# Attention and two feed-forward blocks on one core: when the first block's W34 parts are made, in which order its second products are queued, and where the x splits stand

## The chip, the cores and the metric

The kernel runs on one NeuronCore of one Trainium2 chip, as one program. The metric is the device time in microseconds. The kernel before took 2330.16 us, the median of 3 runs (2330.05 to 2332.1).

TensorE (PE in the profile) multiplies; VectorE (DVE), ScalarE (ACT) and GpSimd (POOL) split, add and evacuate; the sync engine (SP) issues the DMAs.

## The reference

```python
x = attention(q, k, v, tau)             # 4 x 8 heads, 576 tokens, 64 wide -> 2304 tokens x 512
x = ((x @ w1) * (x @ w2)) @ w3 @ w_out  # first block, weights in float64
P = sinkhorn(exp(x @ w_gate))           # 8 rounds, 2304 x 8
out = sum over e of P[:, e] * (relu(x @ e1[e]) @ e2[e])   # 8 experts, 512 -> 1024 -> 512
```

The kernel multiplies `w3 @ w_out` once beforehand and calls the result W34. The first block is then `((x @ w1) * (x @ w2)) @ W34`.

## The kernel before, in words

**Split numbers.** Each fp32 operand of a product is split into two fp32r parts, high and low (`xh`/`xl`, `w1h`/`w1l`, `w2h`/`w2l`, `hh`/`hl`). A product of two split operands is three matmuls: high by high, high by low, low by high. The high part is a copy on ACT, the low part a subtraction on DVE or POOL.

**Units.** The tokens are three superblocks of 768. The first block (24 units) goes superblock by superblock, eight units each: a, b, a, b, ... An a-unit is a quarter of `x @ w1`, the b-unit behind it the same quarter of `x @ w2`. Units are numbered from 0, so even ones are a and odd ones b; units 8, 16 and 24 open a superblock, and what happens around them is called a turn here. From unit 24 on there are 96 expert units of the same build.

**Slots.** A unit has seven slots (Strassen-Winograd). In each, `mm1` issues six matmuls of 384 columns into one of two PSUM banks (`px` for slots 0, 2, 4, `py` for 1, 3, 5, 6), then `pop` issues some second products, then `evac`/`combine` reads the bank: p, u, v and three or four results. In an a-unit the results stay in `ca`. In a b-unit each result c is multiplied by `ca` (the "product c", L652), ACT copies its high part `hh` and DVE makes its low part `hl` (L654). These steps wait in `self.later` and are issued one and two slots after, the last three behind slot 6.

**Second products.** At the end of a b-unit `queue_b` queues its 48 matmuls with W34: 24 of 256 columns into two `ye` banks, then 24 of 512 columns into four others. `pop` spreads them over the 16 shares of the next a- and b-unit (slot 5 has two shares). PE executes all of this in the order of issue.

**W34's parts.** `prep2` makes `w2h` on ACT at slot 3 and `w2l` on DVE (L566) at slot 5, and then issues the load of the next raw piece but one. In the first block it is called in the b-unit, for that unit's own quarter.

**x splits.** At a turn the seven `xh`/`xl` pairs of the next superblock are made by `xsplit` (L585 on ACT, L586 on DVE). `SPLITS_AT` says behind which slot: positions 0 to 6 are the slots of the last unit, 7 to 13 those of the first unit of the next superblock. Split number k is used first by slot k of that unit, at position 7 + k.

**POOL** makes the next unit's `w1` parts in each unit: L531, L534, L537, L538, L541 and, longest, L543.

Of the kernel before, what the change touches and what calls it, by code (L numbers as in the profile page):

```python
# [24 lines left out]
SB = 768  # L25
# [2 lines left out]
QW = 2 * S + 128  # L28

SPLITS_AT = ((0, 0), (1, 1), (2, 2), (3, 3), (8, 4), (9, 5), (10, 6))  # L30

CONVERT = (1, 1, 1, 1, 1, 1, 1, 1, 0, 1, 1, 2, 2, 1, 1, 2, 1, 1)
PRODUCTS = (0, 1, 0, 1, 4, 0, 4, 2, 1, 1, 3, 1, 0, 3, 0, 3, 3, 3)
# [8 lines left out]
def f32(ap):  # L42
    return ap.bitcast(F32)
# [422 lines left out]
class Moe:  # L466
# [87 lines left out]
        self.raw2[u] = raw  # L554

    def prep2(self, u, part):
        if u not in self.raw2:
            return
        if part == 0:
            wh = self.pool2.tile([128, 2, DM], F32R, tag="w2h", name=f"w2h{u}", bufs=2)  # L560
            self.nc.scalar.activation(wh, self.raw2[u], AF.Copy)
            self.w2[u] = [wh]
        else:
            raw = self.raw2.pop(u)
            wl = self.pool2.tile([128, 2, DM], F32R, tag="w2l", name=f"w2l{u}", bufs=2)
            self.nc.vector.tensor_tensor(out=wl, in0=raw, in1=f32(self.w2[u][0]), op=ALU.subtract)  # L566
            self.w2[u].append(wl)
            self.load2()
# [101 lines left out]
    def queue_b(self, u):  # L670
        kind, s, j = self.units[u]
        hh, hl = self.hs.pop(u)
        wh, wl = self.w2.pop(u)
        prods = ((wh, hh), (wh, hl), (wl, hh))
        for m in range(2):
            for n in (2 * m, 2 * m + 1):
                out = self.yb[4 + m][:, 256 * (n % 2):256 * (n % 2) + 256]
                for f in range(2):
                    for i, (w, h) in enumerate(prods):
                        self.mm2(out, w[:, f, 128 * n:128 * n + 128], h[:, f, 0:256],  # L680
                                 j == 0 and n % 2 == 0 and f == 0 and i == 0, j == 3 and n % 2 == 1 and f == 1 and i == 2)
            if j == 3:
                self.queue.append((0, lambda m=m: self.nc.vector.tensor_copy(
                    self.x[:, 2 * m:2 * m + 2, SB * s:SB * s + 256],
                    self.yb[4 + m].rearrange("p (a b) -> p a b", a=2))))
        for n in range(4):
            for f in (1, 0):
                for i, (w, h) in enumerate(prods):
                    self.mm2(self.yb[n], w[:, f, 128 * n:128 * n + 128], h[:, f, 256:SB],
                             j == 0 and f == 1 and i == 0, j == 3 and f == 0 and i == 2)  # L690
            if j == 3:
                self.queue.append((0, lambda n=n: self.nc.scalar.activation(
                    self.x[:, n, SB * s + 256:SB * s + SB], self.yb[n], AF.Copy)))
# [44 lines left out]
    def gate(self, s, slot):  # L738

        ps = self.xy[0 if slot == 6 else 1]  # L740
        t0 = slot - 2
        for tc in (t0, t0 + 1):
            t = SB * s + 128 * tc
            for d in range(4):
                self.nc.tensor.matmul(ps[:, E * tc:E * tc + E], lhsT=self.x[:, d, t:t + 128], rhs=self.wg[:, d],
                                      start=d == 0, stop=d == 3, skip_group_check=True)

        def out():
            self.nc.scalar.activation(self.p[:, 6 * s + t0:6 * s + t0 + 2],
                                      ps[:, E * t0:E * t0 + 2 * E].rearrange("p (a b) -> p a b", a=2), AF.Copy)  # L750
        return out
# [34 lines left out]
    def run(self):  # L786
        units = self.units
        self.load1(0)
        self.load1(1)
        prep = self.prep1(0)  # L790
        for slot in range(7):
            if slot < 4:
                self.xsum(0, slot, self.nc.vector)
            self.xsplit(0, slot)
            if slot >= PD:
                next(prep, None)
            yield
        for _ in prep:
            pass
        sink = None  # L800
        gates = {8 * s + (12 if s + 1 < NSB else 9): s for s in range(NSB)}
        for u, (kind, s, j) in enumerate(units):
            nxt = units[u + 1] if u + 1 < len(units) else None
            while u == 1 and self.pool2 is None:
                yield
            if kind != "a":
                self.hs[u] = tuple(self.pool2.tile([128, 2, SB], F32R, tag=t, name=f"{t}{u}", bufs=2)
                                   for t in ("hh", "hl"))
            ahead = [units[min(u + i, len(units) - 1)][1] for i in range(5)]
            splits = dict(SPLITS_AT) if ahead[1] != s else {}  # L810
            if u and units[u - 1][1] != s:
                splits = {at - 7: slot for at, slot in SPLITS_AT}
            prep = self.prep1(u + 1)
            self.load1(u + 2)
            for slot in range(7):
                yield
                late, self.late = self.late[:2], self.late[2:]
                self.mm1(u, slot)
                gate = self.gate(gates[u], slot) if u in gates and slot in (2, 4, 6) else None
                self.pop(slot)  # L820
                if sink:
                    try:
                        sink.send(self.xy[1 if slot < 4 else 0])
                    except StopIteration:
                        sink = None
                self.evac(u, slot)
                if gate:
                    gate()
                    if u == 8 * NSB + 1 and slot == 6:
                        sink = self.sinkhorn()  # L830
                        next(sink)
                for f in late:
                    f()
                if slot in splits:
                    self.xsplit(ahead[1], splits[slot])
                next(prep, None)
                if slot == 5 and ahead[4] != s:
                    self.xsum(ahead[4], next(i for i in range(4) if ahead[3 - i] == s), self.nc.gpsimd)
                if slot in (3, 5):
                    self.prep2(u, (slot - 3) // 2)  # L840
            while self.later:
                self.later.pop(0)()
            if kind == "b":
                self.queue_b(u)
                self.left = (2 if nxt[0] == "a" else 1) * (6 + SHARE)
            elif kind != "a":
                self.queue_d(u)
                self.left = 6 + SHARE
        self.left = 0
        self.pop(6)  # L850
        for f in self.late:
            f()
# [61 lines left out]
```

## Time and profile before

| | us |
|---|---|
| span of the profiled execution | 2331.0 |
| its time | 2332.75 |
| median of the runs | 2330.16 |
| PE busy | 2247.0 (96%) |
| DVE busy | 1283.8 (55%) |
| ACT busy | 999.3 (43%) |
| POOL busy | 1179.2 (51%) |

The profiled execution is itself a run of the kernel, 2.59 us above the median of the others. A busy PE is an upper bound, since matmuls are pipelined and their ends are modelled: where rows follow each other, the distance of their starts is the pace. In the trace a wait stands in brackets behind the instruction that waited, with what ended it. The first block runs from about 474 to 805 us; the last second products of it end in the unit that starts at 804.72 us.

### The profile page before, as it was taken

The numbers are of one execution on the slowest core, as the hardware profiler recorded it, in microseconds if no ns is written. First come the engines' busy times: TensorE is split into PE (matmuls) and PEld (weight loads), VectorE is DVE, ScalarE is ACT, GpSimd is POOL, SyncE is SP. The second block draws the span as 40 slices with busy tenths as digits, with TensorE's granted clock in tenths as the row PEclk, the third lists the DMA queues.
The fourth block names the chain that finished last, engine by engine and source line by source line (L and its number), as shares of the span: only waits on it lengthen the run. The fifth ranks groups of instructions, "written<-read, shape, count | busy, mean of one in ns | idle before, by whom it ended". The sixth has DMA issues, their size and how long they took to land.

```text
span 2331.0 us, 32170 instructions
## 1 busy us (share of the span) xinstructions
PE 2247.0 (96%) x12544; PEld 2053.2 (88%) x12544; DVE 1283.8 (55%) x2207; ACT 999.3 (43%) x1853; POOL 1179.2 (51%) x1093
## 2 busy tenths in 40 slices
PE   6999999988989899999999999999999999999999
PEld 6899999878888888999999999999999899999998
DVE  6888888665555655544444644444444634444444
ACT  5877877633333333333333433333333443333332
POOL 3655555376666644444445644444446544444441
PEclk8999999989999999999999999999999999999999
DMA  5334443111111111221111121211221222112211
GB/s 141 101 117 122 122 125 116 62 69 70 64 51 59 46 55 55 73 73 66 61 73 73 69 86 73 73 65 63 73 73 59 95 73 73 64 64 73 73 61 48
DMA packets 52824, 177.73 MB, mean 76 GB/s; under 512 B 6592, under 2 KB 6592, under 8 KB 52672
## 3 DMA queue, kind: packets, MB, share of 16 engines
q1 hardware_dynamic: 52672, 175.68, 22.5%
q8 instruction: 98, 1.61, 0.3%
q14 instruction: 54, 0.44, 0.1%
HBM read 164.64 MB, written 11.01 MB: 75 GB/s over the span
## 4 chain that ended last, share of the span: by engine, by line
PE 87%; DVE 8%; issue 2%; ACT 2%; DMA 0%; SPq 0%; DVEq 0%; ACTq 0%
PE ye L667 37%; PE py L597 20%; PE px L597 15%; PE pv L225 4%; PE s L138 4%; PE t L183 2%; PE w L424 2%; DVE xl L586 1%; DVE nmx L143 1%; DVE c L652 1%; DVE p L158 1%; PE vs L207 1%; PE xt L239 1%; PE tt L194 0%; DVE c L641 0%
## 5 line engine op out<-in xcount | busy, mean ns | idle before, releaser
L543 POOL TENSOR_TENSOR w1l<-wt,w1h 128x1024 fp32r<-128x1024 f32 x120 | 290.8, 2423 | 326.3 <-ACT w1h L540 326.3
L667 PE MATMUL ye<-w2h,hl 128*128 128x512 f32 x1152 | 452.4, 393 | 0.0
L667 PE MATMUL ye<-w2h,hh 128*128 128x512 f32 x1152 | 451.5, 392 | 0.0
L667 PE MATMUL ye<-w2l,hh 128*128 128x512 f32 x1152 | 450.8, 391 | 0.0
L662 ACT ACTIVATE hh<-c 128x384 fp32r<-128x384 f32 x288 | 151.4, 526 | 615.0 <-DVE c L641 614.9
L538 POOL TENSOR_TENSOR w1l<-raw,w1h 128x256 fp32r<-128x256 f32 x120 | 92.0, 766 | 515.1 <-ACT w1h L532 515.1
L597 PE MATMUL py<-xh,w1h 128*128 128x384 f32 x960 | 325.3, 339 | 17.8 <-DVE c L641 12.2
L597 PE MATMUL py<-xh,w1l 128*128 128x384 f32 x960 | 324.1, 338 | 0.4 <-POOL w1l L543 0.4
L597 PE MATMUL py<-xl,w1h 128*128 128x384 f32 x960 | 324.3, 338 | 0.0
L597 PE MATMUL px<-xh,w1h 128*128 128x384 f32 x720 | 243.8, 339 | 3.7 <-DVE hl L663 3.4
L667 PEld LDWEIGHTS ye<-w2h,hl 128*128 128x128 f32 x1152 | 216.5, 188 | 32.5
L667 PEld LDWEIGHTS ye<-w2l,hh 128*128 128x128 f32 x1152 | 216.4, 188 | 32.5
L597 PE MATMUL px<-xh,w1l 128*128 128x384 f32 x720 | 243.1, 338 | 0.0
L597 PE MATMUL px<-xl,w1h 128*128 128x384 f32 x720 | 243.1, 338 | 0.0
L667 PEld LDWEIGHTS ye<-w2h,hh 128*128 128x128 f32 x1152 | 216.5, 188 | 24.0
L597 PEld LDWEIGHTS py<-xh,w1h 128*128 128x128 f32 x960 | 181.1, 189 | 43.1 <-DVE c L641 15.6
L597 PEld LDWEIGHTS py<-xl,w1h 128*128 128x128 f32 x960 | 181.5, 189 | 17.9
L624 DVE TENSOR_TENSOR u<-py,p 128x384 f32<-128x384 f32 x120 | 66.8, 556 | 215.9 <-PE py L597 215.0
L597 PEld LDWEIGHTS py<-xh,w1l 128*128 128x128 f32 x960 | 181.7, 189 | 0.9 <-POOL w1l L543 0.9
L531 POOL TENSOR_TENSOR wt<-raw 128x512 f32<-128x512 f32 x120 | 162.9, 1358 | 27.3 <-DMA raw<-w_a 12.3
L663 DVE SCALAR_TENSOR_TENSOR hl<-c,hh 128x384 fp32r<-128x384 f32 x288 | 164.6, 572 | 9.5
L662 ACT ACTIVATE hh<-px 128x384 fp32r<-128x384 f32 x96 | 47.4, 494 | 274.7 <-PE px L597 274.7
(138 smaller groups left out, 4584.7 us busy)
## 6 DMA issues: line engine op xcount, KB each, us to landing
raw<-in_e SPq DMA_DIRECT2D x192, 512.0 KB, 4.0
r<-in_qk SPq DMA_DIRECT2D x60, 288.0 KB, 5.7
wraw<-in_w SPq DMA_DIRECT2D x32, 512.0 KB, 4.0
raw<-w_a SPq DMA_DIRECT2D x12, 512.0 KB, 4.4
raw<-w_b SPq DMA_DIRECT2D x12, 512.0 KB, 3.2
raw<-w SPq DMA_DIRECT2D x12, 512.0 KB, 3.6
rv<-in_vv SPq DMA_DIRECT2D x16, 320.0 KB, 4.3
out<-acc SPq DMA_DIRECT2D x18, 256.0 KB, 2.0
```

The source lines that it names most:

```text
L138: nc.tensor.matmul(ps[:, c, 0:288], lhsT=qs[:, q0:q0 + 128], rhs=kk[:, h, cols], start=i == 0, stop=i == len(ops) - 1)
L183: nc.tensor.transpose(ps[:, c], p[:, 128 * c:128 * c + 128], k.ident)
L225: nc.tensor.matmul(outs[g][:, bs, 0:64], lhsT=l[:, i] if i < 4 else tail, rhs=rv[:, hs, i] if i < 4 else rv[0:65, hs, 4], start=i == 0, st ...
L424: nc.tensor.matmul(self.ps, lhsT=a[:, 128 * (kc % 4):128 * (kc % 4) + 128], rhs=b[:, kc], start=j == 0, stop=j == 23)
L531: nc.gpsimd.tensor_tensor(out=t[:, 0:2], in0=raw[:, 1:3], in1=raw[:, 0:2], op=ALU.subtract)
L538: nc.gpsimd.tensor_tensor(out=wl[:, 0], in0=raw[:, 0], in1=f32(wh[:, 0]), op=ALU.subtract)
L543: nc.gpsimd.tensor_tensor(out=wl[:, 3:7], in0=t, in1=f32(wh[:, 3:7]), op=ALU.subtract)
L597: self.nc.tensor.matmul(out, lhsT=w[:, wi, o], rhs=x[xi][:, d], start=n == 0 and not adds, stop=n == 5, skip_group_check=True)
L624: tt(out=self.u2, in0=py, in1=self.p1, op=ALU.add)
L662: nc.scalar.activation(hi, src, AF.Relu)
L663: self.later.append(lambda: nc.vector.scalar_tensor_tensor(out=lo, in0=src, scalar=0.0, in1=f32(hi), op0=ALU.max, op1=ALU.subtract))
L667: self.queue.append((out.shape[-1], lambda: self.nc.tensor.matmul(out, lhsT=l, rhs=r, start=start, stop=stop, skip_group_check=True)))
```

## The change

Four edits, all in the first block.

1. `FIRST_SPLITS_AT` takes the place of `SPLITS_AT` at the three turns that follow a b-unit: the seven splits move from positions 0, 1, 2, 3, 8, 9, 10 to 4, 6, 7, 8, 9, 10, 11.
2. In an a-unit `prep2` makes the W34 parts of the b-unit behind it. In that b-unit the call finds nothing left to do. (Unit 0 runs before the pool for these parts exists, so unit 1 makes its own, as before.)
3. `queue_b` queues the 256-column products by half f, then by high-high, low-high, high-low, and inside by the four output blocks n; the 512-column products of f = 1 likewise, those of f = 0 by block, as before.
4. The two copies of finished x columns (L683) are queued together, behind all 24 of the 256-column products.

```diff
--- before.py
+++ after.py
@@ -28,6 +28,8 @@
 QW = 2 * S + 128
 
 SPLITS_AT = ((0, 0), (1, 1), (2, 2), (3, 3), (8, 4), (9, 5), (10, 6))
+
+FIRST_SPLITS_AT = ((4, 0), (6, 1), (7, 2), (8, 3), (9, 4), (10, 5), (11, 6))
 
 CONVERT = (1, 1, 1, 1, 1, 1, 1, 1, 0, 1, 1, 2, 2, 1, 1, 2, 1, 1)
 PRODUCTS = (0, 1, 0, 1, 4, 0, 4, 2, 1, 1, 3, 1, 0, 3, 0, 3, 3, 3)
@@ -554,7 +556,7 @@
         self.raw2[u] = raw
 
     def prep2(self, u, part):
-        if u not in self.raw2:
+        if u not in self.raw2 or part and u not in self.w2:
             return
         if part == 0:
             wh = self.pool2.tile([128, 2, DM], F32R, tag="w2h", name=f"w2h{u}", bufs=2)
@@ -671,23 +673,24 @@
         kind, s, j = self.units[u]
         hh, hl = self.hs.pop(u)
         wh, wl = self.w2.pop(u)
-        prods = ((wh, hh), (wh, hl), (wl, hh))
-        for m in range(2):
-            for n in (2 * m, 2 * m + 1):
-                out = self.yb[4 + m][:, 256 * (n % 2):256 * (n % 2) + 256]
-                for f in range(2):
-                    for i, (w, h) in enumerate(prods):
-                        self.mm2(out, w[:, f, 128 * n:128 * n + 128], h[:, f, 0:256],
-                                 j == 0 and n % 2 == 0 and f == 0 and i == 0, j == 3 and n % 2 == 1 and f == 1 and i == 2)
-            if j == 3:
+        prods = ((wh, hh), (wl, hh), (wh, hl))
+        for f in range(2):
+            for i, (w, h) in enumerate(prods):
+                for n in range(4):
+                    out = self.yb[4 + n // 2][:, 256 * (n % 2):256 * (n % 2) + 256]
+                    self.mm2(out, w[:, f, 128 * n:128 * n + 128], h[:, f, 0:256],
+                             j == 0 and n % 2 == 0 and f == 0 and i == 0, j == 3 and n % 2 == 1 and f == 1 and i == 2)
+        if j == 3:
+            for m in range(2):
                 self.queue.append((0, lambda m=m: self.nc.vector.tensor_copy(
                     self.x[:, 2 * m:2 * m + 2, SB * s:SB * s + 256],
                     self.yb[4 + m].rearrange("p (a b) -> p a b", a=2))))
+        for i, (w, h) in enumerate(prods):
+            for n in range(4):
+                self.mm2(self.yb[n], w[:, 1, 128 * n:128 * n + 128], h[:, 1, 256:SB], j == 0 and i == 0, False)
         for n in range(4):
-            for f in (1, 0):
-                for i, (w, h) in enumerate(prods):
-                    self.mm2(self.yb[n], w[:, f, 128 * n:128 * n + 128], h[:, f, 256:SB],
-                             j == 0 and f == 1 and i == 0, j == 3 and f == 0 and i == 2)
+            for i, (w, h) in enumerate(prods):
+                self.mm2(self.yb[n], w[:, 0, 128 * n:128 * n + 128], h[:, 0, 256:SB], False, j == 3 and i == 2)
             if j == 3:
                 self.queue.append((0, lambda n=n: self.nc.scalar.activation(
                     self.x[:, n, SB * s + 256:SB * s + SB], self.yb[n], AF.Copy)))
@@ -807,9 +810,11 @@
                 self.hs[u] = tuple(self.pool2.tile([128, 2, SB], F32R, tag=t, name=f"{t}{u}", bufs=2)
                                    for t in ("hh", "hl"))
             ahead = [units[min(u + i, len(units) - 1)][1] for i in range(5)]
-            splits = dict(SPLITS_AT) if ahead[1] != s else {}
-            if u and units[u - 1][1] != s:
-                splits = {at - 7: slot for at, slot in SPLITS_AT}
+            splits = {}
+            if ahead[1] != s:
+                splits = dict(FIRST_SPLITS_AT if kind == "b" else SPLITS_AT)
+            elif u and units[u - 1][1] != s:
+                splits = {at - 7: slot for at, slot in (FIRST_SPLITS_AT if units[u - 1][0] == "b" else SPLITS_AT)}
             prep = self.prep1(u + 1)
             self.load1(u + 2)
             for slot in range(7):
@@ -837,7 +842,7 @@
                 if slot == 5 and ahead[4] != s:
                     self.xsum(ahead[4], next(i for i in range(4) if ahead[3 - i] == s), self.nc.gpsimd)
                 if slot in (3, 5):
-                    self.prep2(u, (slot - 3) // 2)
+                    self.prep2(u + 1 if kind == "a" else u, (slot - 3) // 2)
             while self.later:
                 self.later.pop(0)()
             if kind == "b":
```

On PE, after slot 0 of unit 18 (`px`) come the second products of unit 17 and then slot 1 (`py`). Before:

```order
L597 MATMUL px<-xh_5691,w1h_7594 128x384
L597 MATMUL px<-xl_5698,w1h_7594 128x384
L597 MATMUL px<-xh_5691,w1l_7595 128x384
L667 MATMUL ye_5869<-hh_7580,w2h_7638 128x256
L667 MATMUL ye_5869<-hl_7581,w2h_7638 128x256
L667 MATMUL ye_5869<-hh_7580,w2l_7668 128x256
L667 MATMUL ye_5869<-hh_7580,w2h_7638 128x256
L667 MATMUL ye_5869<-hl_7581,w2h_7638 128x256
L597 MATMUL py<-xh_5695,w1h_7594 128x384
```

With the change (lines are two further down):

```order
L599 MATMUL px<-xh_5691,w1h_7599 128x384
L599 MATMUL px<-xl_5698,w1h_7599 128x384
L599 MATMUL px<-xh_5691,w1l_7600 128x384
L669 MATMUL ye_5869<-hh_7585,w2h_7541 128x256 x2
L669 MATMUL ye_5870<-hh_7585,w2h_7541 128x256 x2
L669 MATMUL ye_5869<-hh_7585,w2l_7572 128x256
L599 MATMUL py<-xh_5695,w1h_7599 128x384
L599 MATMUL py<-xl_5702,w1h_7599 128x384
L599 MATMUL py<-xh_5695,w1l_7600 128x384
```

The fifth product, which read the low part `hl` of half 1, reads `w2l` now; the first product that reads `hl` is the ninth, and it reads half 0.

On DVE, from product c of slot 4 of unit 17 (a b-unit) on; u belongs to unit 18. Before:

```order
L652 TENSOR_TENSOR c_17_4_7650<-c_4_7648,ca 128x384
L566 TENSOR_TENSOR w2l_7668<-raw_17_7237,w2h_7638 128x1024
L641 TENSOR_TENSOR c_6_7680<-py,u_17_1_7607 128x384
L652 TENSOR_TENSOR c_17_5_7664<-c_5_7662,ca 128x384
L654 TENSOR_TENSOR hl_7581<-c_17_4_7650,hh_7580 128x384
L652 TENSOR_TENSOR c_17_6_7682<-c_6_7680,ca 128x384
L654 TENSOR_TENSOR hl_7581<-c_17_5_7664,hh_7580 128x384
L654 TENSOR_TENSOR hl_7581<-c_17_6_7682,hh_7580 128x384
L624 TENSOR_TENSOR u_18_1_7722<-py,p_18_0_7703 128x384
```

With the change:

```order
L654 TENSOR_TENSOR c_17_4_7652<-c_4_7650,ca 128x384
L643 TENSOR_TENSOR c_6_7679<-py,u_17_1_7612 128x384
L654 TENSOR_TENSOR c_17_5_7667<-c_5_7665,ca 128x384
L656 TENSOR_TENSOR hl_7586<-c_17_4_7652,hh_7585 128x384
L654 TENSOR_TENSOR c_17_6_7681<-c_6_7679,ca 128x384
L656 TENSOR_TENSOR hl_7586<-c_17_5_7667,hh_7585 128x384
L656 TENSOR_TENSOR hl_7586<-c_17_6_7681,hh_7585 128x384
L626 TENSOR_TENSOR u_18_1_7722<-py,p_18_0_7703 128x384
L629 TENSOR_TENSOR v_3_7751<-py,u_18_1_7722 128x384
L639 TENSOR_TENSOR ca<-px,v_3_7751 128x384
L639 TENSOR_TENSOR ca<-py,v_3_7751 128x384
L568 TENSOR_TENSOR w2l_7782<-raw_19_7351,w2h_7755 128x1024
```

`w2l` has left the b-unit; the next b-unit's stands in the a-unit, between `ca` of slot 5 and `ca` of slot 6.

On DVE, the end of unit 15, the last of a superblock. Before, from product c of slot 2:

```order
L657 TENSOR_TENSOR c_15_2_7399<-px,ca 128x384
L586 TENSOR_TENSOR xl_5699<-x,xh_5692 128x768
L627 TENSOR_TENSOR v_3_7414<-py,u_15_1_7385 128x384
L654 TENSOR_TENSOR hl_7357<-c_15_2_7399,hh_7356 128x384
L586 TENSOR_TENSOR xl_5701<-s_5705,xh_5694 128x768
L641 TENSOR_TENSOR c_4_7431<-px,v_3_7414 128x384
L641 TENSOR_TENSOR c_5_7445<-py,v_3_7414 128x384
L652 TENSOR_TENSOR c_15_4_7433<-c_4_7431,ca 128x384
L566 TENSOR_TENSOR w2l_7451<-raw_15_7002,w2h_7421 128x1024
L641 TENSOR_TENSOR c_6_7463<-py,u_15_1_7385 128x384
L652 TENSOR_TENSOR c_15_5_7447<-c_5_7445,ca 128x384
L654 TENSOR_TENSOR hl_7357<-c_15_4_7433,hh_7356 128x384
```

With the change, from c of slot 4 on:

```order
L643 TENSOR_TENSOR c_4_7427<-px,v_3_7414 128x384
L588 TENSOR_TENSOR xl_5698<-x,xh_5691 128x768
L643 TENSOR_TENSOR c_5_7443<-py,v_3_7414 128x384
L654 TENSOR_TENSOR c_15_4_7429<-c_4_7427,ca 128x384
L643 TENSOR_TENSOR c_6_7457<-py,u_15_1_7389 128x384
L654 TENSOR_TENSOR c_15_5_7445<-c_5_7443,ca 128x384
L656 TENSOR_TENSOR hl_7363<-c_15_4_7429,hh_7362 128x384
L588 TENSOR_TENSOR xl_5702<-s_5706,xh_5695 128x768
L654 TENSOR_TENSOR c_15_6_7459<-c_6_7457,ca 128x384
L656 TENSOR_TENSOR hl_7363<-c_15_5_7445,hh_7362 128x384
L656 TENSOR_TENSOR hl_7363<-c_15_6_7459,hh_7362 128x384
L588 TENSOR_TENSOR xl_5699<-x,xh_5692 128x768
```

Of the four splits that the unit held, the one of slot 0 stands behind c of slot 4 now, the one of slot 1 in the tail behind slot 6, and the next behind the tail; `w2l` is gone from the unit.

## Rows read from the trace of the kernel before

**Rows 1.** The page's chain of work that ended last, by engine.
```profile
PE 87%; DVE 8%; issue 2%; ACT 2%; DMA 0%; SPq 0%; DVEq 0%; ACTq 0%
```

**Rows 2.** Waits of PE, 494 to 823 us: waiter, releaser: total us, times, longest.
```profile
PE ye L667 <- DVE hl L654: 15.3, 12, 1.5
...
PE ye L667 <- DVE w2l L566: 5.6, 9, 1.2
```

**Rows 3.** Six a-units: us; busy us of PE, PEld, DVE, ACT, POOL; clock; DMA.
```profile
546.07:562.59 16.52, 13.85 (x76) 13.12 (x74) 8.62 (x13) 4.22 (x8) 11.82 (x9) 0.90 0.27 95
...
717.23:730.88 13.65, 12.22 (x75) 11.69 (x74) 7.03 (x12) 4.17 (x8) 9.69 (x8) 1.00 0.32 116
...
sum 90.47, PE 78.48 PEld 74.46 DVE 46.84 ACT 25.12 POOL 65.03; mean PE 13.08 PEld 12.41 DVE 7.81 ACT 4.19 POOL 10.84
```

**Rows 4.** Timeline of PE at unit 18: start us, us, instruction, [idle before].
```profile
717.23 0.34 PE L597 MATMUL px<-xh,w1h 128*128 128x384 f32 x1
...
718.27 0.28 PE L667 MATMUL ye<-hh,w2h 128*128 128x256 f32 x1
...
718.62 0.28 PE L667 MATMUL ye<-hh,w2h 128*128 128x256 f32 x1
720.33 0.39 PE L667 MATMUL ye<-hl,w2h 128*128 128x256 f32 x1 [1.43 <-DVE hl L654]
...
722.19 0.34 PE L597 MATMUL px<-xh,w1h 128*128 128x384 f32 x1
```

**Rows 5.** Timeline of DVE, end of unit 17 and start of unit 18.
```profile
715.94 2.32 DVE L566 TENSOR_TENSOR w2l<-raw,w2h 128x1024 fp32r<-128x1024 f32 x1
718.19 0.55 DVE L641 TENSOR_TENSOR c<-py,u 128x384 f32<-128x384 f32 x1
718.66 0.62 DVE L652 TENSOR_TENSOR c<-c,ca 128x384 f32<-128x384 f32 x1
719.20 1.07 DVE L654 TENSOR_TENSOR hl<-c,hh 128x384 fp32r<-128x384 f32 x1
720.31 0.56 DVE L652 TENSOR_TENSOR c<-c,ca 128x384 f32<-128x384 f32 x1
720.78 1.23 DVE L654 TENSOR_TENSOR hl<-c,hh 128x384 fp32r<-128x384 f32 x2
```

**Rows 6.** Timeline of ACT there.
```profile
720.90 0.53 ACT L653 ACTIVATE hh<-c 128x384 fp32r<-128x384 f32 x1 [1.07 <-DVE c L652]
721.33 0.47 ACT L621 ACTIVATE p<-px 128x384 f32<-128x384 f32 x1
```

**Rows 7.** Units 2, 15, 16 and 17 as windows, columns as in rows 3.
```profile
494.07:510.52 16.45, 14.05 (x75) 13.32 (x75) 8.36 (x13) 4.21 (x8) 10.85 (x9) 0.90 0.28 96
674.74:688.96 14.22, 11.50 (x59) 10.12 (x58) 10.71 (x13) 7.23 (x11) 9.96 (x7) 1.00 0.00 0
688.96:706.26 17.30, 14.29 (x75) 13.23 (x74) 13.57 (x17) 6.54 (x12) 11.14 (x9) 0.90 0.27 92
706.26:717.23 10.97, 10.97 (x60) 10.20 (x59) 5.22 (x9) 5.23 (x9) 6.05 (x5) 1.00 0.00 1
```

**Rows 8.** Timeline of all engines across the turn from unit 15 to 16.
```profile
677.24 0.96 DVE L586 TENSOR_TENSOR xl<-x,xh 128x768 fp32r<-128x768 f32 x1 [2.19 <-ACT xh L585]
...
687.35 0.45 PE L597 MATMUL py<-xh,w1h 128*128 128x384 f32 x1 [2.24 <-DVE c L641]
...
694.43 0.83 ACT L585 ACTIVATE xh<-s 128x768 fp32r<-128x768 f32 x1
...
700.39 2.40 POOL L543 TENSOR_TENSOR w1l<-wt,w1h 128x1024 fp32r<-128x1024 f32 x1 [2.93 <-ACT w1h L540]
...
700.60 3.00 DVE L586 TENSOR_TENSOR xl<-x,xh 128x768 fp32r<-128x768 f32 x1
...
704.46 0.68 DVE L683 COPY x<-ye 128x512 f32<-128x512 f32 x1
...
704.68 0.41 PE L597 MATMUL py<-xh,w1h 128*128 128x384 f32 x1 [1.15 <-DVE ca L637]
```

## Prediction

> **What bounds the kernel now.** Read the chain of waits on the page first: PE makes 87% of it [rows 1]. So a change beside PE pays only by what PE waits for. The waits of PE in the first block come next: they name the low part `hl` twelve times (15.3 us) and `w2l` nine times (5.6 us) [rows 2], both ahead of second products. Then cut the block into units. Five a-units of the plain kind are alike in work, but last from 13.65 to 17.86 us; six together take 90.47 us, and the one at 546.07 us runs at a granted clock of 0.90, the one at 717.23 us at 1.00 [rows 3]. The b-unit behind it has no wait: 10.97 us long, PE busy for 10.97 [rows 7].
>
> Where the a-unit loses its time is in the timeline of PE [rows 4]. Six products of 384 columns take 718.27 - 717.23 = 1.04 us, 0.173 each; three of 256 columns take 718.62 - 718.27 = 0.35, 0.115 each. The fifth second product should start at 718.74 and starts at 720.33: 1.59 us late (1.43 in the row's bracket; the rest is the modelled end). Without it unit 18 would last 13.65 - 1.59 = 12.06 us. It waits for the `hl` of half 1, which stands on DVE behind `w2l` (2.32 us), c and a product c and ends at 719.20 + 1.07 = 720.27 [rows 5].
>
> **The plain a-units.** Edit 3 takes both waits from there: the fifth product reads `w2l` now, made a unit earlier, and `hl` of half 1 is read first by product 21, in slot 4, some 6 us later. Six ungated plain a-units take 90.47 us; at 12.06 each they would take 72.36: 18.1 us, the clock's share included. Two more (units 12 and 20, with gate matmuls) have a mean `hl` wait, 15.3/12 = 1.28 + 0.16 = 1.44 each: 2.9. Together 21.0 us.
>
> What is late next: p of slot 0, which ACT makes behind the last `hh`. From c of slot 6 (718.19) to the end of p (721.33 + 0.47) are 3.61 us [rows 5, 6]. Without `w2l` in front, c can start when slot 6's products are done, two 512-column products before 717.23, near 717.0; so p ends near 720.6. Slot 2, which overwrites p's bank, would start at 722.19 - 1.59 = 720.60 [rows 4]. The cover is gone, just: I charge 0.3 us per unit, between 0 (POOL out of the way of `hl`, which then takes less than 1.07) and 0.9 (each DVE step as long as that `hl`). Eight units: -2.4, bounds 0 and -7.2.
>
> `w2l` goes to slot 5 of the a-unit, where only `ca` of slot 6 stands behind it on DVE. At 2.32 us, its price beside POOL, it starts after `ca` of slot 5 and ends some 3 us after that slot's products; `ca` must be read before slot 1 of the b-unit, which is more than 4 us after them (slot 5's share of two, slot 6, slot 0 and their second products). Hidden, with about 0.5 us to spare. `w2h` moves from one slot 3 to the other on ACT: only p of the next unit is behind it, hidden too. SP issues the raw load behind `w2l` a unit earlier, hence before the next unit's `w1` load instead of after it; the buffer is free by then, and PE waits for no DMA here: nothing. That consecutive second products alternate between two banks costs nothing: PE goes from `px` to `ye` at full pace already [rows 4].
>
> **Unit 2** lasts 16.45 us, 4.4 over 12.06 [rows 7]. Unit 1 still makes its own `w2l`, at the same place, so that wait stays; p takes the place of the `hl` wait. Only the clock, 0.90 there, can come back: 16.45 x 0.10 = 1.65, say +1.8 with the little that p is earlier than `hl`.
>
> **The turns.** Units 15 and 16 last 14.22 + 17.30 = 31.52 us; undisturbed they would be 10.97 + 12.06. So a turn loses 8.5 us now [rows 7], the 2.24 and 1.15 us waits of slot 6 [rows 8] and a clock of 0.90 (1.7 us) in it. With the change, step by step:
> - Slot 6 of the last unit: one split in front of c of slot 5 instead of four: 0 to 2.0, I take 0.9.
> - The second split. Behind slot 6 stand c (0.47 to the next start), a product c (0.54), `hl` (1.07) [rows 5], then `xl` (0.96 [rows 8]): 3.0 us. PE needs it after two 512-column products (0.43), slot 0 (1.04), five second products (0.58) and one product (0.17): 2.2. So 0.8 us late, and 2.8 if the split of slot 4, ahead of all this, takes 3.00 instead of 0.96; I take 1.8.
> - The third split, from there: a product c (0.56), `hh` (0.53), p (0.47), `xh` (0.83), `xl` (0.96): 3.35 us [rows 5, 6, 8]; PE has the rest of slot 1 (0.86) and 0.75 more before it needs it: 1.7 late.
> - The next three: 0.96 each against 1.62 per slot: 0 to 0.8, I take 0.4.
> - The last split meets L543 again, as it does now: 0 to 1.3, I take 1.3.
> - The two copies (0.68 each) and `w2l` in front of the last `ca`: 0 to 1.3, I take 0.5.
> - The clock: 0 or 1.7; I take 1.7.
>
> That is 8.3 us, between 2.5 and 11.6, against 8.5: +0.2 per turn, +0.6 for three (between +18 and -9). The third turn, into the experts, is put at the same.
>
> The 0.96 and 3.00 are one instruction. The long one started 0.21 us behind POOL's L543 (2.40 us) and ended 0.81 us after it [rows 8]. The Trainium skill (SBUF — State Buffer, "Who interferes with whom") says that a VectorE instruction with two SBUF inputs and a GpSimd instruction that reads SBUF exclude each other for a whole instruction, and that the order of issue decides who blocks. The trace agrees: 3.00 against 0.96 us. By that rule each split that starts within L543 costs up to 2.40 more, which speaks against any move that puts more of them there; the slower rival below is that.
>
> **The sum.** 21.0 - 2.4 + 1.8 + 0.6 = 21.0 us. The profiled time, 2332.75, becomes 2311.75. That execution lay 2.59 above the median of the runs, so the forecast is 2309 us.
>
> **The rivals.**
> - The turns come out clean: the splits find DVE idle, no clock is lost. Unit 15's DVE is busy for 10.71 of 14.22 us and unit 16's for 13.57 of 17.30 [rows 7], much of that blocked time; against it stands the third split's chain through ACT, of which 1.7 us is hard to hide. +18 instead of +0.6: 2292.
> - The wait only changes its name: p, or u behind it, holds slot 2 or 3 by 0.9 us in all eight units, and the turns cost 11.6. For it: the 3.61 us chain. 21.0 - 7.2 + 1.8 - 9.3 = 6.3: 2324.
> - Slower: at the turns the splits run into POOL. With four of the seven at 3.00 instead of 0.96 and PE waiting for each (two slots of lead, no cushion), a turn loses 8.2 more: 21.0 - 2.4 + 1.8 + 0.6 - 24.5 = -3.5, so 2334. It decides from 6.4 us more per turn on. For it: 3.00 of today's `xl` [rows 8]; against it: POOL has one L543 per unit, so few of the seven can meet it.
> - The change does not do what it says: what waits in the a-unit is DVE's tail as a whole, and PE stops one slot later for as long. About 2329. Against it: the five first products need nothing of that tail.
>
> **How the numbers follow.** The forecast 0.56 (its own range 2302 to 2317), clean turns 0.17, renamed waits 0.16, slower 0.07, no effect 0.04. The range goes to 2296 and 2323, most of the way to the first two rivals. A measurement of this kernel can tell 0.2%, 4.7 us, from no change. Faster: the first three cases but for a part of the renamed waits, 0.86; within 0.2%: 0.06; slower 0.08.
>
> **What would show it.** After: no wait of PE on `hl` L656 or `w2l` L568 in the plain a-units, and these at 12.0 to 12.5 us with a clock of 1.00; a short wait on ACT's p in slot 2, if any; at the turns waits on `xl` in slots 1 and 2 of the new superblock's first unit. Wrong would be: plain a-units above 13 us, or a turn (last unit and the one behind it) above 35 us.

## The result, and the profile after

The changed kernel took 2310.58 us (median of 4 runs, 2305.85 to 2311.1), beside 2331.13 us for the kernel before on the same chip: a ratio of 0.9911, 95% interval 0.9897 to 0.9925. Two later measurements gave 0.9929 (0.9911 to 0.9947) and 0.9920 (0.9908 to 0.9933). The forecast was 2309, with a range of 2296 to 2323. The profiled execution took 2310.22 us (span 2308.1); the sum had 2311.75 for it.

Where the time came from is seen by cutting the trace at the same instruction in both kernels: from the first matmul of unit 2 to the first of unit 25. First the kernel before (columns as in [rows 3]: us; busy us of PE, PEld, DVE, ACT, POOL; clock; DMA):

```profile
494.07:821.89 327.82, 296.46 (x1640) 276.48 (x1639) 186.37 (x253) 115.56 (x203) 214.25 (x153) 0.96 0.16 57
```

And the changed kernel:

```profile
490.95:797.39 306.44, 286.87 (x1639) 266.15 (x1639) 181.39 (x253) 114.15 (x201) 217.53 (x153) 1.00 0.18 61
```

That stretch is 327.82 - 306.44 = 21.4 us shorter; the sum had 21.0. What precedes it, in which the kernels are alike, was 3.1 us shorter in this execution, and what follows 1.6 us longer; so two executions differ. PE's busy time over the same matmuls fell by 296.46 - 286.87 = 9.6 us and the clock rose from 0.96 to 1.00: by this reckoning somewhat under half of the gain is the clock, the rest are shorter waits. Whole executions agree: in group 4 below, those with the same mean clock of 0.989 took 2327.24 to 2329.03 us before the change and, the only one, 2315.33 with it, 12 to 14 us less.

The waits of PE from 490 to 797.5 us, after (waiter, releaser: total us, times, longest), answer to [rows 2]:

```profile
PE px L599 <- ACT p L623: 6.3, 8, 1.5
PE py L599 <- DVE c L643: 3.3, 5, 0.7
PE py L599 <- ACT xh L587: 2.8, 3, 1.1
PE py L599 <- DVE xl L588: 2.6, 4, 0.7
PE py L599 <- DVE ca L639: 1.9, 2, 1.0
PE px L599 <- DVE xl L588: 1.7, 3, 0.6
...
PE ye L669 <- DVE w2l L568: 0.7, 1, 0.7
```

`hl` is gone from the list and `w2l` is down to unit 2's 0.7 us. The first place belongs to p, on ACT, and the waits on `xh` and `xl` are new.

The six ungated plain a-units, with the sum over them, answer to [rows 3]:

```profile
539.92:553.60 13.68, 12.23 (x75) 11.70 (x74) 8.42 (x13) 5.17 (x9) 11.24 (x8) 1.00 0.00 0
...
699.59:712.11 12.52, 12.21 (x75) 11.67 (x74) 7.46 (x12) 6.51 (x12) 8.89 (x8) 1.00 0.01 2
...
sum 78.31, PE 73.37 PEld 70.15 DVE 47.50 ACT 33.58 POOL 61.23; mean PE 12.23 PEld 11.69 DVE 7.92 ACT 5.60 POOL 10.21
```

They take 78.31 instead of 90.47 us, all at full clock. Of these 12.16 us, 78.48 - 73.37 = 5.1 are PE's busy time, which is the clock, and 7.1 are waits. The one at 699.59 us is unit 18. PE there, against [rows 4]:

```profile
699.59 0.34 PE L599 MATMUL px<-xh,w1h 128*128 128x384 f32 x1
...
701.22 0.34 PE L599 MATMUL py<-xh,w1h 128*128 128x384 f32 x1
...
703.32 0.44 PE L599 MATMUL px<-xh,w1h 128*128 128x384 f32 x1 [0.31 <-ACT p L623]
```

Slot 1 starts 701.22 - 699.59 = 1.63 us after slot 0 (3.32 before); in front of slot 2 stands the wait on p. The tail on DVE and then ACT, against [rows 5] and [rows 6]:

```profile
699.90 0.56 DVE L643 TENSOR_TENSOR c<-py,u 128x384 f32<-128x384 f32 x1 [0.46 <-DVE c L654]
700.37 0.90 DVE L654 TENSOR_TENSOR c<-c,ca 128x384 f32<-128x384 f32 x1
701.20 0.54 DVE L656 TENSOR_TENSOR hl<-c,hh 128x384 fp32r<-128x384 f32 x1
701.78 0.56 DVE L654 TENSOR_TENSOR c<-c,ca 128x384 f32<-128x384 f32 x1
```

```profile
702.37 0.53 ACT L655 ACTIVATE hh<-c 128x384 fp32r<-128x384 f32 x1
702.80 0.47 ACT L623 ACTIVATE p<-px 128x384 f32<-128x384 f32 x1
```

`w2l` no longer stands in front of c. From c at 699.90 to the end of p at 703.27 are 3.37 us; PE wanted the bank 0.47 us before it got it.

Units 2, 15, 16 and 17 against [rows 7]:

```profile
490.95:505.63 14.68, 12.74 (x75) 11.80 (x75) 9.93 (x14) 5.16 (x9) 11.43 (x9) 1.00 0.20 71
659.45:671.42 11.97, 11.23 (x59) 10.20 (x58) 7.14 (x9) 3.53 (x7) 9.53 (x8) 1.00 0.38 131
671.42:688.61 17.19, 13.53 (x75) 11.71 (x74) 14.38 (x19) 9.56 (x15) 11.77 (x9) 1.00 0.00 1
688.61:699.59 10.98, 10.98 (x59) 10.16 (x58) 6.09 (x9) 3.39 (x7) 7.87 (x6) 1.00 0.41 143
```

Units 15 and 16 together take 29.16 us instead of 31.52. Their timeline, POOL, DVE and PE, against [rows 8]:

```profile
665.83 2.64 POOL L545 TENSOR_TENSOR w1l<-wt,w1h 128x1024 fp32r<-128x1024 f32 x1 [2.29 <-ACT w1h L542]
...
667.16 2.13 DVE L588 TENSOR_TENSOR xl<-x,xh 128x768 fp32r<-128x768 f32 x1
...
669.81 0.45 PE L599 MATMUL py<-xh,w1h 128*128 128x384 f32 x1 [0.74 <-DVE c L643]
...
674.30 0.45 PE L599 MATMUL py<-xh,w1h 128*128 128x384 f32 x1 [1.09 <-ACT xh L587]
...
675.41 0.45 PE L599 MATMUL py<-xl,w1h 128*128 128x384 f32 x1 [0.67 <-DVE xl L588]
...
677.55 0.45 PE L599 MATMUL px<-xh,w1h 128*128 128x384 f32 x1 [0.41 <-ACT xh L587]
...
678.54 0.44 PE L599 MATMUL px<-xl,w1h 128*128 128x384 f32 x1 [0.55 <-DVE xl L588]
...
687.04 0.41 PE L599 MATMUL py<-xh,w1h 128*128 128x384 f32 x1 [0.95 <-DVE ca L639]
```

The first split (667.16) lasts 2.13 us, since POOL runs L545 from 665.83 to 668.47, and c of slot 5 is late by 0.74 us in the bracket. Then PE waits for `xh` and `xl` of the second split (1.09 and 0.67), of the third (0.41 and 0.55), and for `ca` (0.95).

The third turn, into the experts, is another matter. Unit 24 after:

```profile
777.42:797.39 19.97, 17.17 (x91) 14.66 (x90) 16.37 (x23) 10.64 (x18) 12.46 (x9) 1.00 0.00 1
```

It lasted 17.17 us before. Units 23 and 24 together went from 32.25 to 31.94 us, 0.3 less, while the first two turns gained 2.3 and 2.4 us.

### The profile page after: what moved, and what is told of

Read it like the earlier page. It is cut to its first block, busy times and chain, and to the rows that moved or that the text cites. A ratio compares the mean times of both kernels' runs of the same rounds, so it can differ in the third digit from the quotient of the medians.

```text
span 2308.1 us, 32172 instructions
## 1 busy us (share of the span) xinstructions
PE 2236.2 (97%) x12544; PEld 2040.8 (88%) x12544; DVE 1277.3 (55%) x2207; ACT 999.2 (43%) x1853; POOL 1182.4 (51%) x1093
## 4 chain that ended last, share of the span: by engine, by line
PE 67%; DVE 2%; ACT 0%; issue 0%; POOL 0%; DVEq 0%
PE ye L669 35%; PE py L599 18%; PE px L599 14%; DVE c L654 1%; DVE xl L588 0%; DVE c L643 0%; PE py L748 0%; ACT xh L587 0%; DVE prob L777 0%; PE px L748 0%; DVE hl L656 0%; DVE hl L665 0%; DVE acc L723 0%; DVE prob L784 0%; DVE small L775 0%
## 5 line engine op out<-in xcount | busy, mean ns | idle before, releaser
L545 POOL TENSOR_TENSOR w1l<-wt,w1h 128x1024 fp32r<-128x1024 f32 x120 | 292.9, 2440 | 314.8 <-ACT w1h L542 314.7
L533 POOL TENSOR_TENSOR wt<-raw 128x512 f32<-128x512 f32 x120 | 166.5, 1388 | 26.8 <-ACT xh L587 12.1
```

The source lines that it names most:

```text
L533: nc.gpsimd.tensor_tensor(out=t[:, 0:2], in0=raw[:, 1:3], in1=raw[:, 0:2], op=ALU.subtract)
L545: nc.gpsimd.tensor_tensor(out=wl[:, 3:7], in0=t, in1=f32(wh[:, 3:7]), op=ALU.subtract)
```

## The experiments

Two quantities of each trace are compared below besides the time, both from the starts of the units' first matmuls: the six ungated plain a-units together, and the six units at the turns (7, 8, 15, 16, 23, 24) together. "Block" is the stretch from unit 2 to unit 25. The kernels of a group ran side by side on one chip, with the kernel before; the groups 2, 3 and 4 ran on three different chips. The change itself ran in groups 1, 3 and 4, so in group 2 it is compared through the ratio and the trace.

| kernel | ratio to before (95%) | median us | six a-units | six turn units | block |
|---|---|---|---|---|---|
| before, groups 1 to 4 | | 2331.1, 2328.4, 2329.6, 2329.0 | 90.5 | 95.3 | 327.8 |
| the change, group 1 | 0.9911 (0.9897 to 0.9925) | 2310.6 | 78.3 | 90.3 | 306.4 |
| again, group 3 | 0.9929 (0.9911 to 0.9947) | 2312.8 | 78.3 | 90.3 | 306.4 |
| again, group 4 | 0.9920 (0.9908 to 0.9933) | 2310.5 | 78.4 | 92.6 | 308.8 |
| without edit 1, group 2 | 0.9892 (0.9876 to 0.9909) | 2305.8 | 78.2 | 87.2 | 304.0 |
| without edit 1, group 4 | 0.9903 (0.9889 to 0.9916) | 2306.5 | 78.2 | 87.1 | 303.9 |
| without edit 3, group 2 | 0.9945 (0.9927 to 0.9962) | 2318.4 | 79.2 | 94.2 | 311.9 |
| without edit 2, group 2 | 0.9998 (0.9987 to 1.0009) | 2329.3 | 85.0 | 97.6 | 325.6 |
| edit 2 alone, group 4 | 0.9916 (0.9903 to 0.9930) | 2310.8 | 79.2 | 87.7 | 306.8 |
| x sums in a-units, group 2 | 0.9893 (0.9874 to 0.9911) | 2304.5 | 74.5 | 89.2 | 301.5 |
| late low part, group 3 | 0.9905 (0.9888 to 0.9922) | 2306.6 | 75.5 | 92.8 | 304.7 |
| three early splits, group 3 | 0.9911 (0.9894 to 0.9927) | 2307.7 | 78.2 | 85.6 | 301.7 |
| all three, group 3 | 0.9867 (0.9848 to 0.9886) | 2298.3 | 71.8 | 84.9 | 293.1 |
| sums, low part, old splits, group 4 | 0.9877 (0.9863 to 0.9890) | 2299.7 | 71.8 | 88.7 | 296.9 |

### Edit 1 undone

```diff
-FIRST_SPLITS_AT = ((4, 0), (6, 1), (7, 2), (8, 3), (9, 4), (10, 5), (11, 6))
+FIRST_SPLITS_AT = SPLITS_AT
```

> The change without its first edit: the x splits stand at the old positions at all three turns. Theory (the plain a-units carry the gain, the splits little): units 15 and 16 together last 29.5 to 31 us against 29.2 with the change and 31.5 before, the wait of 2.2 us on c of slot 5 is back in unit 15, and no xh or xl wait stands in unit 16; the time is 0 to 5 us above the change, 2311 to 2316 us. Rival (the later splits are the larger part): the turns fall back to 8.5 us lost each and more, 2318 us or above.

Units 15 and 16 of this kernel:

```profile
660.42:674.64 14.22, 11.51 (x59) 10.13 (x58) 10.46 (x13) 6.28 (x10) 10.88 (x8) 1.00 0.33 111
674.64:688.97 14.33, 12.47 (x75) 11.62 (x74) 13.11 (x16) 6.80 (x12) 10.52 (x9) 1.00 0.01 1
```

Unit 15 is as long as before the change (14.22), but unit 16 lasts 14.33 instead of 17.19 us with the change: no split is late there. Unit 24, 19.97 us long with the change, has no wait of PE left:

```profile
780.26:796.11 15.85, 15.85 (x91) 14.58 (x90) 14.40 (x20) 7.99 (x15) 11.78 (x9) 1.00 0.00 1
```

The turns cost 3.1 us less than with the later splits: 0.6 each at the first two, of which 0.4 each come back in units 9 and 17, and 1.9 at the third. So what edit 1 costs lies mostly at the turn into the experts. The theory had the waits right (2.2 us on c of slot 5 are back, none on `xh` or `xl` in unit 16) and the direction wrong: it had units 15 and 16 at 29.5 us or more, they take 28.55, and the kernel is faster without this edit, not slower. Once more, beside the change on one chip (group 4):

> The change without its first edit (old split positions) once more, beside the change on one chip. Theory from the two traces (the later splits cost 2.4 us: the six units at the turns last 87.2 instead of 90.3 us, units 9 and 17 0.4 more each): 1.5 to 4 us faster than the change. Rival (the difference seen between two chips was the chips'): within 1 us of the change, or slower.

> The changed kernel itself, for the comparison on this chip: 0.990 to 0.993 of the kernel before.

2306.49 us (2305.74 to 2309.03) beside 2310.51 (2307.89 to 2315.33), 4.0 us apart, though the intervals of the two ratios overlap; the blocks of the traces are 303.86 and 308.75. Two traces of each kernel ran the whole block at full clock: 304.0 and 303.9 us without edit 1, 306.4 and 306.4 with it. So the later splits cost some 2.4 us in an execution in which the clock holds, and edit 1 is a loss. In the change's own execution on this chip one of the first two turns was worse; unit 8 and unit 16, same columns as above:

```profile
563.70:583.19 19.49, 16.27 (x76) 14.13 (x74) 15.69 (x19) 9.55 (x15) 12.44 (x9) 0.82 0.00 0
671.83:689.03 17.20, 13.53 (x76) 11.72 (x75) 14.39 (x19) 9.56 (x15) 11.79 (x9) 1.00 0.00 1
```

The same instructions took 19.49 us at a granted clock of 0.82 in one, and 17.20 at 1.00 in the other. The 0.82 is a mean: part of unit 8 ran at the lower of the clock's two levels, with products of 384 columns 0.32 us apart instead of 0.173. That the later splits bring this on is not shown. In the two traces without edit 1 no turn lost the clock, but with the old positions the kernel before lost it at each of its three turns, and so did the kernel of the last experiment below; with the later ones, two traces of the change kept it throughout and the third lost it once.

### Edit 3 undone

Edit 4 is undone with it, so what follows is the worth of both together.

```diff
-        prods = ((wh, hh), (wl, hh), (wh, hl))
-        for f in range(2):
-            for i, (w, h) in enumerate(prods):
-                for n in range(4):
...
+        prods = ((wh, hh), (wh, hl), (wl, hh))
+        for m in range(2):
+            for n in (2 * m, 2 * m + 1):
...
```

> The change without its third edit: the second products are queued in the old order, the W34 parts are still made a unit sooner. Theory (DVE's tail behind a b-unit bounds the a-unit, whoever waits for it): a wait on hl of 0.5 to 1.5 us returns in slot 0 of the a-units and the wait on p in slot 2 shrinks by as much; plain a-units last 12.4 to 12.9 us, those behind a unit with an x sum 13.6 to 14.0; the time is 0 to 5 us above the change, 2311 to 2316. Rival (as the prediction has it, the order is what takes the hl waits away): 1.4 us per a-unit come back, 2322 to 2328 us.

Waits of PE in its block:

```profile
PE ye L669 <- DVE hl L656: 10.3, 12, 1.5
PE py L599 <- DVE xl L588: 6.1, 6, 1.9
```

The waits on `hl` are back, but in place of the waits on p: the six a-units take 79.2 us, 0.9 more than with the change. That part is the theory's. The turns are not: 94.2 against 90.3 us, with waits on `xl` of up to 1.9 us and a clock of 0.91 in unit 16. The time, 2318.4, lies between the two theories' ranges. The ratio, 0.9945 (0.9927 to 0.9962), is above all three of the change's, 0.9911 to 0.9929, but its interval meets two of theirs. By the trace the order of the queue, with edit 4, is worth little in the plain units and some 4 us at turns with late splits.

### Edit 2 undone

```diff
-                    self.prep2(u + 1 if kind == "a" else u, (slot - 3) // 2)
+                    self.prep2(u, (slot - 3) // 2)
```

> The change without its second edit: each b-unit makes its own W34 parts, w2l stands in front of c of slot 6 again. Theory (the 2.3 us of w2l in the tail are what mattered): p ends some 1 to 1.4 us later in every a-unit, which PE waits for in slot 2, besides a w2l wait in slot 0 of some; plain a-units last 13.4 to 15 us and the turns 2 us more: 2322 to 2332 us. Rival (the order of the queue alone takes the waits away): below 2316 us.

```profile
PE px L599 <- ACT p L623: 7.9, 9, 1.2
...
PE ye L669 <- DVE w2l L568: 5.2, 7, 0.9
```

Nothing is left of the gain: 0.9998 (0.9987 to 1.0009). Without edit 2 the other edits turn a wait on `hl` into waits on p (7.9 us) and `w2l` (5.2). In this trace units 8 and 16 ran at a clock of 0.83 and the block at 0.96; the six a-units, at full clock, take 85.0 us, 6.7 more than with the change. The theory held. With `w2l`, edit 2 also moves `w2h` and the load of the raw piece; no run separates them, but `w2l` is the one that stood in the tail [rows 5].

### Edit 2 alone

Both diffs of the edits 1 and 3 above together.

> The second edit alone: W34's parts made a unit sooner, with the old order of the queue and the old split positions. Theory (w2l out of the tail is the main part; the order of the queue adds some 0.2 to 0.5 us per a-unit and spares units 8, 16 and 24 more): a wait on hl of 0.5 to 1.4 us in the a-units, 2308 to 2316 us, 1 to 6 us above the change. Rival (each edit needs the other, as the edits 1 and 3 alone brought nothing): 2320 us or above.

```profile
PE ye L669 <- DVE hl L656: 8.9, 12, 1.5
```

Unit 2 of this kernel:

```profile
494.40:510.69 16.29, 13.86 (x75) 13.12 (x75) 10.00 (x14) 5.16 (x9) 11.44 (x9) 0.90 0.17 64
```

The one line of edit 2 gives the whole gain: 2310.76 us beside the change's 2310.51, and a block of 306.8 beside 306.4; the 1 to 6 us above the change that were expected are not there. With edits 3 and 4 on top the block is 303.9 (the kernel without edit 1). Of these 2.9 us, 1.6 are unit 2, which ran at a clock of 0.90 here and takes 14.7 us there; with the same old queue it kept the clock in the run of edit 3 undone (14.90 us), so that part may be chance. Some 1.3 us are left for edits 3 and 4, and edit 1 costs 2.4.

### The x sums moved out of the b-units

POOL makes the four x sums of a turn (`xsum`), one in each of the last four units of a superblock, behind L545. In the changed kernel, at the end of unit 13, POOL, DVE and PE:

```profile
643.79 1.85 POOL L580 TENSOR_TENSOR s<-s,x 128x768 f32<-128x768 f32 x1
...
644.03 2.03 DVE L654 TENSOR_TENSOR c<-c,ca 128x384 f32<-128x384 f32 x1
...
650.64 0.44 PE L599 MATMUL px<-xh,w1h 128*128 128x384 f32 x1 [1.45 <-ACT p L623]
```

The product c (644.03) takes 2.03 us beside the sum, where the ones in [rows 5] take 0.62 and 0.56, and unit 14 then waits 1.45 us for p, not 0.3. The edit:

```diff
+                sums = {(4, 2): 3, (4, 5): 0, (6, 2): 1, (6, 5): 2}
+                if u < 8 * NSB:
+                    if (u % 8, slot) in sums:
+                        self.xsum((s + 1) % NSB, sums[u % 8, slot], self.nc.gpsimd)
-                if slot == 5 and ahead[4] != s:
+                elif slot == 5 and ahead[4] != s:
```

> The change, and POOL's four x sums of a turn moved out of the b-units in front of it: sums 3 and 0 in unit 4 of a superblock (slots 2 and 5), sums 1 and 2 in unit 6. Theory (where the wait on p is 1.5 us rather than 0.3, an x sum on POOL held up the product c of slot 4 on DVE): the wait on p falls from 1.45 to 0.2 to 0.5 us in units 6, 14 and 22, and the turns shorten by 0.5 to 1.5 us: 4 to 8 us faster than the change, 2303 to 2307 us. Rival (the longer wait belongs to these units' own work and not to POOL): 1.4 us stay and the time is within 2 us of the change.

The same unit 14, and the sum over the six a-units:

```profile
643.83:656.21 12.38, 12.22 (x75) 11.70 (x74) 7.60 (x11) 5.05 (x9) 9.97 (x8) 1.00 0.01 2
...
sum 74.46, PE 73.37 PEld 70.16 DVE 45.50 ACT 33.24 POOL 58.00; mean PE 12.23 PEld 11.69 DVE 7.58 ACT 5.54 POOL 9.67
```

12.38 instead of 13.68 us, and units 6 and 22 alike; the block is 4.9 us shorter than the change's. The sum on POOL was the cause of the longer wait, though not by that one product alone. The end of unit 13 on DVE in this run:

```profile
642.09 1.59 DVE L654 TENSOR_TENSOR c<-c,ca 128x384 f32<-128x384 f32 x1
...
644.26 0.55 DVE L654 TENSOR_TENSOR c<-c,ca 128x384 f32<-128x384 f32 x1
```

The same product still takes 1.59 us, now beside L533, which POOL runs there in the sum's place. The two products behind it take 0.55 and 0.56 us instead of 0.99 and 0.98, since POOL's next instructions, no longer pushed back by the sum, stand elsewhere. The three together give the 1.3 us.

### The low part of slot 4 issued later

```diff
-        for f in todo:
+        hold = todo[1:] if kind == "b" and slot == 6 else []
+        for f in todo[:1] if hold else todo:
             f()
+        self.later += hold
...
-                c2 = tmp("c2", 2)
-                ca = self.ca[:, i]
+                c2 = ca = self.ca[:, i]
```

> The changed kernel itself, once more, so that what follows is compared on one chip. Every theory: 0.987 to 0.993 of the kernel before, 2305 to 2312 us.

> The change, and in the tail of a b-unit the low part of slot 4 is issued behind the product c of slot 6 instead of ahead of it (the products c are written in place into ca, so that no third buffer is needed). Theory (what PE waits for in slot 2 is the chain c, product c, low part, product c, last hh, p): p ends 0.5 to 1.1 us sooner; the p wait is gone from the a-units where it was 0.3 and falls from 1.45 to 0.3 to 0.9 in units 6, 14 and 22; 2 to 7 us faster than the change. Rival (p waits for something else on ACT, or the low part is then late for product 21): within 2 us of the change, or slower with a wait on hl.

```profile
PE px L599 <- ACT p L625: 2.0, 5, 0.6
```

The wait on p falls from 6.3 to 2.0 us, and the six a-units from 78.3 to 75.5. 2306.56 us (2305.94 to 2308.32) beside the change's 2312.75 (2309.08 to 2314.71): 6.2 us, as the theory had it, though the intervals of the two ratios overlap. In its trace two turns lost the clock (unit 8, 19.51 us at 0.83, and unit 16, 17.44 at 0.90), so the block shows only 1.8 us of it. The change itself lies just above the 2312 us expected of it. The product c in place is part of this edit; the later low part is not tried without it.

### Three early splits

```diff
-FIRST_SPLITS_AT = ((4, 0), (6, 1), (7, 2), (8, 3), (9, 4), (10, 5), (11, 6))
+FIRST_SPLITS_AT = ((0, 0), (1, 1), (2, 2), (8, 3), (9, 4), (10, 5), (11, 6))
```

> The change with three splits at their old early places and the others two slots ahead of use: positions 0, 1, 2, 8, 9, 10, 11. Theory (the splits in and behind the tail are late because the tail is in front of them; the first three cost nothing where they stood, the fourth met L545 and an x sum): the waits on xh and xl in slots 1 and 2 of units 8, 16 and 24 go, p's wait takes their place with 0.7 us, a wait of 0.7 on v may be back in slot 5 of units 7, 15 and 23; the turns last 26 to 28 us instead of 29.2: 3 to 8 us faster than the change. Rival (early splits cost what late ones do): within 2 us of the change.

```profile
661.45:674.52 13.07, 11.50 (x60) 10.12 (x59) 9.30 (x12) 5.56 (x9) 10.47 (x8) 1.00 0.36 120
674.52:689.16 14.64, 12.97 (x76) 11.64 (x75) 13.07 (x17) 7.52 (x13) 10.75 (x9) 1.00 0.01 1
```

Units 15 and 16 take 27.71 us instead of 29.16, the block is 4.8 us shorter. In time 2307.66 beside 2312.75 us, with intervals that overlap (0.9911, 0.9894 to 0.9927, against 0.9929, 0.9911 to 0.9947): the trace shows it, the times only point the same way.

### All three, and a check of the splits

> Three edits on top of the change: x sums in the a-units, the low part of slot 4 behind the product c of slot 6, and splits at positions 0, 1, 2, 8, 9, 10, 11. Theory (they remove different waits): no p wait in plain a-units, which last 12.1 us, and turns of 25 to 27 us: 11 to 17 us faster than the change, 2292 to 2298 us. Rival (the gains overlap, since one chain carries all): 6 to 9 us faster.

```profile
638.46:650.42 11.96, 11.96 (x75) 11.63 (x74) 7.43 (x11) 5.07 (x9) 10.14 (x8) 1.00 0.01 2
...
sum 71.76, PE 71.76 PEld 69.79 DVE 44.60 ACT 33.34 POOL 58.85; mean PE 11.96 PEld 11.63 DVE 7.43 ACT 5.56 POOL 9.81
```

Every plain a-unit lasts 11.96 us, with PE busy throughout. 2298.32 us (2296.86 to 2298.96), 14.4 below the change on the same chip, and the fastest kernel here: 0.9867 (0.9848 to 0.9886) of before. The block is 293.1, 13.3 shorter than the change's. The first two edits add up in the six a-units (3.8 and 2.8 us alone, 6.5 together), and the three together take more off the time than the 6 to 9 us of the rival; the expected range ended at 2298, just below, and the turns of 27.1 us lie just above the 25 to 27 expected.

With the old split positions instead of the three early ones:

> The x sums in the a-units and the late low part on top of the change, with the old split positions. Theory (three early splits are free, the fourth, at position 3, meets L545 on POOL and holds c of slot 5): unit 15 lasts 14 us or more, 0.3 to 1 us longer than with three early splits, and unit 16 13.4; 2298 to 2302 us. Rival (without the x sum in POOL the fourth split is free as well): 2297 us or below.

2299.72 us, in the expected range. Units 15 and 16:

```profile
654.43:670.03 15.60, 12.48 (x59) 10.77 (x58) 11.40 (x15) 6.36 (x10) 12.38 (x9) 0.94 0.31 101
670.03:682.75 12.72, 12.72 (x75) 12.39 (x74) 9.01 (x15) 6.89 (x11) 7.09 (x5) 0.94 0.00 1
```

They take 15.60 and 12.72 us, against 13.64 and 13.47 with three early splits. Unit 15 is over 14 us, as the theory had it, but by more than its 0.3 to 1 us, and unit 16 is below its 13.4. The clock fell to 0.94 in both, and at the other two turns alike, which is 0.06 x 28.32 = 1.7 us per turn; the two units are 1.2 us longer in sum. So the fourth early split holds up unit 15 even without the sum, but unit 16 gives that back, and by this estimate the old positions would be no slower here without the loss of clock. Whether that split brought the loss on is not shown.

## Why the prediction was right, point by point

**The plain a-units.** Right in place and in what came next, too large in size: 14.6 us for all eight, where 18.6 were forecast. The waits on `hl` and `w2l` are gone and p waits in slot 2. I charged 0.3 us per unit; five of the eight show 0.30 to 0.47 us (distance of the starts), and units 6, 14 and 22 show 1.6, well over the 0.9 I had as the outer bound. The mis-sized term is that -2.4, which measured -6.6: I had the product c at the 0.6 us of unit 17, whose tail has no x sum on POOL beside it, and took one unit for all eight. The experiment with the sums shows it. The kernel before had a sign of it: of the units that the prediction calls alike in work, unit 14 lasted 15.14 us there at full clock, 1.5 more than unit 18, and the forecast took both down to 12.06.

**What takes the waits away.** The step "edit 3 takes both waits from there" was wrong in its attribution. With the old order of the queue the plain units last 79.2 us instead of 78.3: the waits then carry the old name and are as short. Edit 2 alone gives 2310.8 us, and all the others without it give nothing (0.9998). It is the 2.3 us of `w2l` in DVE's tail that were in the way of everything, `hl` and p alike.

**Where `w2l` went.** Hidden, as forecast: no wait on `ca` stands in a plain unit.

**Unit 2** lasts 14.68 instead of 16.45 us: 1.77 against the 1.8 forecast, by the clock, which rose from 0.90 to 1.00. That the change did this is not shown: with edit 2 alone the unit stayed at 0.90, and with the old queue and the later splits it ran at 1.00.

**The turns.** 95.3 to 90.3 us for the six units, 5.0 instead of 0.6. Item by item for units 15 and 16, by the distance of starts: slot 6 of unit 15 0.92 (0.9 forecast), second split 1.25 + 0.94 = 2.2 (1.8), third 0.58 + 0.82 = 1.4 (1.7), the next three nothing (0.4), `ca` 1.14 (1.3), copies and `w2l` nothing (0.5), clock nothing (1.7). The item that failed is the clock, and only in that execution: in group 4 unit 8 lost it. The third turn, put at the same as the others, came to 31.94 us from 32.25: the first two gained 4.7 of the 5.0 us. What I did not see is that the turn's gain belongs to edit 2 and that edit 1, taken alone, costs: I compared the later splits with the kernel before, in which `w2l` stood among them, and never with the old positions without `w2l`, where they are 2.4 us better.

**The sum** came out at 21.4 us for 21.0 by luck, since two misses cancel: the plain a-units gave 14.6 us instead of 18.6 (12.16 in the six, 2.45 in the two gated), the turns 4.4 more than I had. The forecast of the total is better than its parts.

**The rivals.** The renamed wait was half true: p takes 6.6 us, near its price of 7.2, but the turns did not cost what it added. Clean turns, the slower turns and no effect are ruled out by the trace: `xl` waits stand at each turn, one split is 2.13 us long, and the a-units are 12.16 us shorter in sum.

## What to carry to other kernels

When a wait's releaser stands in a tail of short steps on another engine, find the longest step in that tail that nobody there needs and move that; reordering the consumer only gives the wait another name. When several edits come together, price each against the kernel with the others in place: here one line gave the whole gain, two edits together some 1.3 us more in the trace, and one took more than that back. And read one typical unit, then check whether its neighbours have the same company on the other engines.

## What the runs showed of the hardware

- Two DVE instructions with both inputs in SBUF that started beside a POOL instruction ended only after that one: a product c of 0.56 us took 2.03 beside an x sum and ended 0.42 us after it, and a split of 0.96 us took 2.13 beside L545 and ended 0.82 us after it. An addition with one input in PSUM (`ca`, at 655.26 us of the changed kernel) took its usual 0.56 us although L545 ran from 653.51 to 655.91. With the x sum elsewhere on POOL, the three products of the tail gave 1.3 us per unit back.
- The granted clock is not a function of the program alone: units 8 and 16 of one execution of the change, with the same instructions, ran at 0.82 and at 1.00, for 2.3 us of difference. Before the clock fell in unit 8, PE had waited 1.09 and 0.68 us there, and 1.09 and 0.67 us at the same place of unit 16. In two other executions of the same kernel unit 8 ran at 1.00 too. Before the change the block ran at 0.96 and after at 1.00, and that was somewhat under half of the gain.
